# Moving the weight conversion of a fused attention and feed-forward kernel between ScalarE, VectorE and GpSimd, with products of constants at the start

## The chip, the cores and the metric

The kernel runs on one core of one Trainium2 chip. The metric is the device time of one execution in microseconds (us); lower is better. Eleven runs of the kernel before gave a median of 1387.72 us, from 1386.26 to 1390.83 us.

## What is computed

For 8 batches and 8 heads, with 576 tokens and 64 features a head, in float32:

```python
scores = (1/8) * q @ k.T
thresh = max(scores) - tau
scores = where(scores >= thresh, scores, -1e9)
attn   = exp(scores - max(scores)); attn /= sum(attn) + 1e-9
x      = attn @ v              # heads side by side: (8, 576, 512)
xn     = (x - mean(x)) / sqrt(var(x) + 1e-6) * g_ln
out    = x + max(xn @ w_ch1, 0) @ w_ch2    # 512 -> 2048 -> 512
```

The two weights `w_ch1` and `w_ch2` arrive as 64-bit floats (the kernel sees them as 64-bit integers), so the kernel itself turns each of them into float32 before its first use. `g_ln` is multiplied into the rows of `w_ch1`.

## The kernel before, in words

**Slots.** The kernel is one unrolled loop over 72 slots, nine for each batch (`for n in range(NS)`). In a slot, four blocks of 128 x 576 scores are computed on TensorE (`scores`, L393), their negated maxima are taken on VectorE (`exponentials`, L407, two instructions of two blocks), the thresholds are made on GpSimd (L411), the exponentials on ScalarE (L419, four), and VectorE multiplies them with the threshold mask and sums them (`weights`, L426, four, then a reciprocal, L433). The scores lie in two PSUM tiles `sc`, so the scores of the next slot wait for the masks of this one. In the first batch the normalised weights are turned on TensorE with diagonal matrices (`diag` L440 on ScalarE, products `tp` and `tr`, copies `em` and `er` L476 and L499 on ScalarE), and multiplied with v (`pv`, L574 and L584, copied to `x` at L597 and L592). In slots 0 to 2 the next head pair is transposed on VectorE (`turn`, L344, L353, L354, after q was scaled on GpSimd at L341), which waits for the loads of q and k from the SP queue (`load_qk`, L116). Each `tp`, `tr`, `pv`, `p1`, `p2` and `mean` takes one of two PSUM banks of the pool `ps_ff` in turn.

**Feed-forward groups.** The tokens form 16 groups of 288. Group g gets its sums over the heads on GpSimd (`add_feature`, L626), its mean by a product with a constant matrix (`avg_sb`), and its centred x (`xc`, L649, VectorE). Then `first_part` makes 16 hidden tiles of four products each (`p`, then the ReLU `hidden`, L779, on ScalarE), and `second_plain` (group 0) or `second_quarters` (the others) makes the second product. These steps are handed out in four quarters of each slot (`second_part`) by due times, so their place between the attention's products is fixed when the program is built. Group 0 starts at slot 6. In `second_plain`, `add_to_x` multiplies the second product from PSUM with 1/standard deviation on VectorE (L687), and adds x on GpSimd (L688).

**Weight conversion.** The class `Weights` converts 32 chunks of 128 x 512 values: 16 of `w_ch1`, then 16 of `w_ch2`. A chunk has these steps:

- `fetch`: a DMA of 512 KB from the SP queue (L252)
- `begin`: two VectorE instructions on the high words (L272, shift and and; L276, and and or) and two ScalarE instructions (L280, the low word scaled; L284, the square of the high word)
- `carry`: an integer addition of the low word's part on GpSimd (L290)
- `mask`: a VectorE instruction that sets tiny values to zero (L299)
- `end`: for `w_ch1` only, the product with `g_sb` on ScalarE (L312)

The raw and half-made chunks lie in pieces of tiles that are not needed yet (`hidden`, parts of the weights' own room, `et`, `x_room`, `stage`); `piece` and `give` hand them out. One call of `tick` takes one step of each kind: it ends, masks, carries and begins at most one chunk, so a chunk is masked three ticks after its begin. Slots 0 to 2 have two ticks, slots 3 to 5 three, later ones six. `first_part` and `second_plain` do not go on before the chunks that they use have ended.

Of the kernel before, what the change touches and what calls it, by code (L numbers as in the profile page):

```python
# [8 lines left out]
F32 = mybir.dt.float32  # L9
# [9 lines left out]
def kernel(  # L19
# [155 lines left out]
    class Weights:  # L175
# [13 lines left out]
        def __init__(self):  # L189
            self.chunks = [  # L190
                (w1_sb[i][:, c : c + WC], w_ch1[i * 128 : (i + 1) * 128, c : c + WC], i)
                for c in range(0, DF, WC)
                for i in range(NK)
            ] + [
                (
                    w2_sb[:, m, d : d + 4].rearrange("p d c -> p (d c)"),
                    w_ch2[d * 128 : (d + 4) * 128, m * 128 : (m + 1) * 128].rearrange(
                        "(d p) c -> p d c", p=128
                    ),
                    None,  # L200
                )
                for m in range(NK)
                for d in range(0, ND, 4)
            ]
            self.n1 = NK * (DF // WC)
            self.fetched = self.begun = self.carried = self.masked = self.ended = 0
            self.raw, self.made, self.due, self.ticks = {}, {}, [], 2
            flat = lambda t: t.rearrange("p a b -> p (a b)")

            x_room = ffn.tile([128, NK, TOK], F32, tag="x", bufs=3, name="x_room")  # L210
            stage = self.stage = consts.tile([128, 8, WC], F32, name="stage")
            et = att.tile([128, NB, 128], F32, tag="et", bufs=1, name="et0")

            n1 = self.n1
            self.free = []
            for t, n, before in (
                (w2_sb.rearrange("p m d c -> p (m d) c"), ND // 2, lambda p: n1 + 2 * p),  # L220
                (hidden, 4, lambda p: 10),
                (et, 2, lambda p: 2 * n1),
                (x_room, 1, lambda p: 2 * n1),
                (stage, 4, lambda p: 2 * n1),
            ):
                for p in range(n):
                    self.free.append((before(p), -1, flat(t)[:, p * 2 * WC : (p + 1) * 2 * WC]))
# [34 lines left out]
        def begin(self):  # L262
            i = self.begun
            got = self.piece(i, 1) or self.piece(i, -1)
            if got is None:
                return
            self.made[i] = got
            a, y = got[2][:, :WC], got[2][:, WC:]
            self.begun += 1
            self.due.append(self.ticks + 3)  # L270
            au, hi = a.bitcast(U32), self.words(i, U32)[:, :, 1]
            nc.vector.tensor_scalar(  # L272
                out=au, in0=hi, scalar1=3, scalar2=0x3FFFFFFF,
                op0=ALU.logical_shift_left, op1=ALU.bitwise_and,
            )
            nc.vector.scalar_tensor_tensor(  # L276
                out=au, in0=hi, scalar=0xC0000000, in1=au,
                op0=ALU.bitwise_and, op1=ALU.bitwise_or,
            )
# [4 lines left out]
            nc.scalar.activation(y, self.words(i, F32)[:, :, 1], func=AF.Square)  # L284
# [8 lines left out]
        def mask(self):  # L293
            i = self.masked
            self.masked += 1
            got = self.made[i]
            a, y = got[2][:, :WC], got[2][:, WC:]
            dst, _, gi = self.chunks[i]
            nc.vector.scalar_tensor_tensor(  # L299
                out=dst if gi is None else a, in0=y, scalar=(1.0625 * 2.0**-15) ** 2, in1=a,  # L300
                op0=ALU.is_ge, op1=ALU.mult,
            )
            if gi is None:
                self.ended += 1
                self.give(self.made.pop(i))

        def end(self):
            i = self.ended
            self.ended += 1
            dst, _, gi = self.chunks[i]  # L310
            got = self.made.pop(i)
            nc.scalar.mul(dst, got[2][:, :WC], g_sb[:, gi : gi + 1])  # L312
            self.give(got)

        def tick(self):
            self.ticks += 1
            if self.ended < self.masked:
                self.end()
            if self.masked < self.carried and self.due[self.masked] <= self.ticks:
                self.mask()  # L320
            if self.carried < self.begun:
                self.carry()
            if self.begun < self.fetched:
                self.begin()

    def by_blocks(u):

# [71 lines left out]
    def exponentials(n):  # L399


        neg = small.tile([128, 4], F32, tag="neg", name="neg")
        thr = small.tile([128, 4], F32, tag="thr", name="thr")
        es = e_room[(n + 1) % 2 if n < SLOTS else 0]
        for h in range(2):
            i = slice(2 * h, 2 * h + 2)
            nc.vector.tensor_reduce(  # L407
                out=neg[:, i], in_=pairs[h],
                axis=AXL.X, op=ALU.max, negate=True,
            )  # L410
            nc.gpsimd.tensor_scalar(  # L411
                out=thr[:, i], in0=neg[:, i], scalar1=-1.0, scalar2=low_sb,
                op0=ALU.mult, op1=ALU.add,
            )
        run(n, "copy")
        for i in range(4):
            if i == 2:
                yield es, thr
            nc.scalar.activation(es[:, i], blocks[i], func=AF.Exp, bias=neg[:, i : i + 1])  # L419
# [262 lines left out]
        for fn in now:  # L682
            fn()

    def add_to_x(g, m, p2, rb):
        o = ffn.tile([128, TOK], F32, tag="o", bufs=4, name="o")
        nc.vector.tensor_mul(o, p2, rb)  # L687
        nc.gpsimd.tensor_tensor(out=o, in0=o, in1=groups[g][:, m], op=ALU.add)  # L688
        aside.append(lambda: store(nc.vector, g, m, o))

# [111 lines left out]
    def second_plain(g, rb):  # L802
        for m in range(NK):
            p2 = ps_ff.tile([128, TOK], F32, tag="ff", name="p2")
            for d in range(ND):
                while conversion.ended <= conversion.n1 + 4 * m + d // 4:
                    yield 0, 0
                product(
                    p2, lhsT=w2_sb[:, m, d], rhs=hidden[:, d],
                    start=(d == 0), stop=(d == ND - 1),  # L810
                )
                if d < ND - 1:
                    yield 2, 1
            aside.append(lambda m=m, p2=p2: add_to_x(g, m, p2, rb))
            yield 2, 1

    def second_quarters(g, rb):
# [121 lines left out]
    def run(n, i):  # L939
        for fn, args in later_calls.pop((n, i), ()):  # L940
            fn(*args)
# [41 lines left out]
    if w_ch1.dtype == I64:  # L983
        conversion.fetch(4)
    else:
        for i in range(NK):
            nc.sync.dma_start(out=w1_sb[i], in_=w_ch1[i * 128 : (i + 1) * 128])
            nc.scalar.mul(w1_sb[i], w1_sb[i], g_sb[:, i : i + 1])
        for i in range(ND):
            nc.sync.dma_start(  # L990
                out=w2_sb[:, :, i],
                in_=w_ch2[i * 128 : (i + 1) * 128, :].rearrange("p (m c) -> p m c", m=NK),
            )
        conversion.begun = conversion.carried = len(conversion.chunks)
        conversion.masked = conversion.ended = conversion.begun

    turn(0)
    load_v(1)
    for n in range(NS):
        b, s = divmod(n, SLOTS)  # L1000
        ticks = (1, 3, 4)[: 2 + n // 3] if n < 6 else range(1, 7)

        def tick(i):
            if i in ticks:
                conversion.tick()

        run(n, -3)
        scores(b, s)
        run(n, -2)
        run(n, -1)  # L1010
        rest = exponentials(n)
        es, thr = next(rest)
        run(n, 0)
        conversion.fetch(2)
        run_first(stores)
        second_part(n, 0)
        while drops and drops[0][0] is nc.gpsimd:
# [4 lines left out]
        if (n + 1) % SLOTS < HP and u < len(units):  # L1022
            turn(u)
            if u + 1 < len(units):
                load_qk(u + 1)
        if n < SLOTS + HP:
            run_all(aside)
        tick(1)
        run(n, 1)
        second_part(n, 1)  # L1030
        tick(2)
        blocks_go = by_blocks(b * HP)
        diags = weights(es, thr, blocks_go)
# [81 lines left out]
```

## Time and profile before

One execution was profiled: 1387.0 us by the device's clock, and a span of 1385.2 us from its first to its last instruction, so 1.8 us lie around the span.

| | before |
|---|---|
| median of 11 runs | 1387.72 us |
| profiled execution | 1387.0 us, span 1385.2 us |
| TensorE (PE) busy | 1320.6 us, 95% |
| VectorE (DVE) busy | 928.7 us, 67% |
| ScalarE (ACT) busy | 463.4 us, 33% |
| GpSimd (POOL) busy | 606.5 us, 44% |
| chain of work that ended last | PE 83%, DVE 9% |
| starts of the first maxima of slots 0 to 7 | 14.24, 26.27, 37.74, 50.28, 64.52, 78.52, 92.94, 121.73 us |
| starts of those of slots 8 to 12 | 147.26, 166.64, 191.45, 211.47, 230.75 us |

In the views, PE is TensorE's products and PEld its weight loads, L numbers are lines of the kernel, a row of the timeline gives start, duration, engine, line, operation and tiles, and the bracket at its end the idle time before it with what ended it. A window row gives a stretch of the span, its length, and then busy time and number of instructions of PE, PEld, DVE, ACT and POOL, TensorE's granted clock, the DMA engines' busy share and GB/s. A product of this kernel in float32 leaves several records in the trace.

### The profile page before, as it was taken

The page shows a single profiled execution, that of the slowest core. Times are in us where ns is not written, and L with a number is a line of the kernel's source. Part 1 is how long each engine was busy: PE and PEld are TensorE (multiplying, and loading weights), DVE is VectorE, ACT ScalarE, POOL GpSimd, SP SyncE. Part 2 cuts the span into 40 slices and gives each one's busy share as a digit, 9 for nine tenths or more (in the row PEclk, how much of TensorE's full clock was granted, in tenths as well). Part 3 has the DMA queues.
Part 4 walks back from the last instruction along what each step waited for, and adds up shares of the span by engine and source line. Part 5 has one row for each costly group of instructions (what it writes and reads, how often), then busy time and mean ns, then how long its engine had stood idle before and what let it go on. Part 6 is the DMA issues. An engine that isn't in the chain of part 4 may idle for free.

```text
span 1385.2 us, 40405 instructions
## 1 busy us (share of the span) xinstructions
PE 1320.6 (95%) x17360; PEld 991.3 (72%) x17360; DVE 928.7 (67%) x1638; ACT 463.4 (33%) x1003; POOL 606.5 (44%) x807
## 2 busy tenths in 40 slices
PE   4878989999999999999999999999999999999996
PEld 3655655867768696877869687776868677686966
DVE  5997967676776767657776667757776767766211
ACT  3877613232332323232232323323232323323120
POOL 2444444544443544443444455353444445344313
PEclk8999999999999999999999999999999999999998
DMA  9722355447734576447754476445764476444211
GB/s 230 183 77 72 93 142 152 169 145 183 200 132 167 139 200 173 147 143 190 196 160 147 152 196 188 145 143 154 198 187 136 139 186 187 134 160 136 56 17 18
DMA packets 322019, 206.85 MB, mean 149 GB/s; under 512 B 247984, under 2 KB 279472, under 8 KB 313776
## 3 DMA queue, kind: packets, MB, share of 16 engines
q1 hardware_dynamic: 317072, 203.68, 51.0%
q8 instruction: 136, 2.23, 0.7%
q10 hardware_dynamic: 4736, 0.59, 0.4%
q14 instruction: 43, 0.35, 0.1%
q0 software_dynamic: 32, 0.00, 0.0%
HBM read 120.46 MB, written 83.76 MB: 147 GB/s over the span
## 4 chain that ended last, share of the span: by engine, by line
PE 83%; DVE 9%; issue 2%; DMA 2%; ACT 2%; POOL 1%; SPq 1%; POOLq 0%; DVEq 0%; ACTq 0%
PE p L101 35%; PE seg L101 28%; PE sc L393 9%; PE sc L574 8%; DVE e L426 2%; PE sc L584 2%; DVE neg L407 2%; DMA v_in<-in_v_dram 1%; SPq L116 1%; DVE w L272 1%; DVE w L299 1%; PE tp L101 1%; POOL q_in L341 1%; PE mean L101 0%; PE var L101 0%
## 5 line engine op out<-in xcount | busy, mean ns | idle before, releaser
L101 PE MATMUL p<-xc,w 128*64 128x288 f32 x4096 | 519.9, 409 | 13.1 <-ACT hidden L779 5.7
L101 PEld LDWEIGHTS p<-xc,w 128*64 128x64 f32 x4096 | 288.1, 137 | 222.5 <-issue 16.7
L407 DVE TENSOR_REDUCE neg<-sc 128x2 f32<-128x1152 f32 x144 | 188.7, 1352 | 241.9 <-PE sc L393 241.5
L101 PE MATMUL seg<-hidden,w 128*64 128x144 f32 x3840 | 248.3, 287 | 3.8 <-DVE hidden L847 3.8
L101 PEld LDWEIGHTS seg<-hidden,w 128*64 128x64 f32 x3840 | 234.8, 137 | 15.7 <-issue 7.5
L442 POOL TENSOR_SCALAR e<-e,den 128x576 f32<-128x576 f32 x252 | 193.7, 780 | 114.9 <-DVE den L431 114.9
L411 POOL TENSOR_SCALAR thr<-neg,low_sb 128x2 f32<-128x2 f32 x144 | 42.2, 293 | 452.2 <-DVE neg L407 450.2
L426 DVE SCALAR_TENSOR_TENSOR e<-sc,thr,e 128x576 f32<-128x576 f32 x288 | 222.1, 810 | 16.2 <-POOL thr L411 14.5
L779 ACT ACTIVATE hidden<-p 128x288 f32<-128x288 f32 x256 | 106.4, 416 | 323.6 <-PE p L101 323.5
L419 ACT ACTIVATE e<-sc,neg 128x576 f32<-128x576 f32 x288 | 197.6, 753 | 8.5 <-DVE neg L407 8.5
L516 DVE STREAM_TRANSPOSE et<-e 128x1152 f32<-128x1152 f32 x112 | 153.2, 1374 | 18.2 <-POOL e L442 17.8
L393 PE MATMUL sc<-kT,qT 64*64 64x384 f32 (+3 forms) x2048 | 144.8, 412 | 21.4 <-DVE e L426 11.3
L574 PE MATMUL sc<-em,v_in 128*64 128x128 f32 (+1 forms) x2368 | 129.4, 263 | 0.0
L574 PEld LDWEIGHTS sc<-em,v_in 128*64 128x64 f32 x2368 | 122.8, 137 | 7.8
L393 PEld LDWEIGHTS sc<-kT,qT 64*64 64x64 f32 x2048 | 78.0, 136 | 65.7 <-issue 22.8
L101 PE MATMUL seg<-hidden,stage 128*64 128x144 f32 x1920 | 123.3, 287 | 0.0
L101 PEld LDWEIGHTS seg<-hidden,stage 128*64 128x64 f32 x1920 | 117.6, 137 | 2.9 <-issue 2.9
L597 ACT COPY x<-sc 128x128 f32<-128x128 f32 x120 | 31.7, 266 | 251.6 <-PE sc L393 184.7
L847 POOL TENSOR_TENSOR hidden<-hidden 128x576 f32<-128x576 f32 x60 | 84.7, 1426 | 47.8 <-ACT hidden L779 38.2
L862 ACT COPY part<-seg 128x288 f32<-128x288 f32 x75 | 30.2, 403 | 198.4 <-PE seg L101 194.3
L847 DVE TENSOR_TENSOR hidden<-hidden 128x576 f32<-128x576 f32 x60 | 49.2, 854 | 49.1 <-PE seg L101 39.1
L101 PE MATMUL seg<-hidden,e 128*64 128x144 f32 x960 | 65.3, 286 | 0.0
(152 smaller groups left out, 1114.7 us busy)
## 6 DMA issues: line engine op xcount, KB each, us to landing
scr<-et SPq DMA_DIRECT2D x63, 1152.0 KB, 4.9
em<-scr SPq DMA_DIRECT2D x63, 1024.0 KB, 5.7
out_dram<-ot SPq DMA_DIRECT2D x256, 36.0 KB, 3.7
q_in<-in_q_dram SPq DMA_DIRECT2D x124, 72.0 KB, 2.6
k_in<-in_k_dram SPq DMA_DIRECT2D x120, 72.0 KB, 2.9
er<-scr SPq DMA_DIRECT2D x126, 64.0 KB, 5.2
v_in<-in_v_dram SPq DMA_DIRECT2D x28, 256.0 KB, 5.4
w<-in_moe_w_ch_dram SPq DMA_DIRECT2D x10, 512.0 KB, 5.9
```

Source lines behind the costliest of these rows:

```text
L101: nc.tensor.matmul(out[r], lhsT=lhsT[:, r], rhs=rhs, **flags)
L393: nc.tensor.matmul(sc[h][64 * i : 64 * i + 64, at : at + n], lhsT=ql[r] if s == HP else qT[r, half, j * 128 + 64 * i : j * 128 + 64 * i + 64],
L407: nc.vector.tensor_reduce(out=neg[:, i], in_=pairs[h], axis=AXL.X, op=ALU.max, negate=True,)
L411: nc.gpsimd.tensor_scalar(out=thr[:, i], in0=neg[:, i], scalar1=-1.0, scalar2=low_sb, op0=ALU.mult, op1=ALU.add,)
L419: nc.scalar.activation(es[:, i], blocks[i], func=AF.Exp, bias=neg[:, i : i + 1])
L426: nc.vector.scalar_tensor_tensor(out=es[:, i], in0=blocks[i], scalar=thr[:, i : i + 1], in1=es[:, i], op0=ALU.is_ge, op1=ALU.mult, accum_o ...
L442: nc.gpsimd.tensor_scalar(out=es[:, i], in0=es[:, i], scalar1=den[:, i : i + 1], scalar2=1.0, op0=ALU.mult, op1=ALU.mult,)
L516: nc.vector.transpose(et[:, :, 64 * h : 64 * h + 64].rearrange("p n (j c) -> p j n c", j=2), es[:, 2 * h : 2 * h + 2].rearrange("p j (n c) ...
L574: nc.tensor.matmul(dst[64 * h : 64 * h + 64], lhsT=vt[:, h, c, :], rhs=pick(em[:, 2 * j : 2 * j + 2, c], h), start=c == 0 and first, stop= ...
L597: nc.scalar.copy(x_of(2 * b + (s > HP))[:, s % (HP + 1), 128 * j : 128 * j + 128], pv[j])
L779: nc.scalar.activation(hidden[:, d], p1, func=AF.Relu)
L847: eng.tensor_tensor(out=out[at], in0=in0[at], in1=in1[at], op=op)
```

## The change

1. **Order of the conversion.** `tick` is gone. Each slot has a row in the table `BEGUN` with three counts: how many chunks may have begun ahead of the masks of the scores, behind them, and at the slot's end. All chunks begun are carried, masked or scaled together at fixed places of the slot. Slots 0 to 5 begin two chunks each, slots 6 to 8 six each, slot 9 the rest. Before, 15 chunks had begun by the end of slot 5, now 12.
2. **The product with g** moves from ScalarE (L312) to GpSimd (`scale`): a few behind the additions ahead of the masks, and the others between the two threshold instructions of a slot.
3. **Products of constants** on TensorE (`constants`) stand in front of the scores of slots 0 to 4: 22, 26, 8, 8 and 8 products of `avg_sb` and `ident`, into a bank of `ps_ff`, and nobody reads them.
4. **Loads.** In the first four slots two chunks are fetched a slot, behind the loads of q and k; from slot 4 on up to three at two places of a slot (before: two at two places in all slots, the first of them ahead of q and k).
5. **Group 0's second product** is copied from PSUM by ScalarE, and multiplied on VectorE from the copy.

The order of instructions on TensorE is otherwise the same, and from slot 11 on all engines have the same order of instructions as before.

```diff
-        def end(self):
-            i = self.ended
-            self.ended += 1
+        def scale(self):
+            i = self.scaled
+            self.scaled += 1
             dst, _, gi = self.chunks[i]
             got = self.made.pop(i)
-            nc.scalar.mul(dst, got[2][:, :WC], g_sb[:, gi : gi + 1])
+            nc.gpsimd.tensor_scalar(
+                out=dst, in0=got[2][:, :WC], scalar1=g_sb[:, gi : gi + 1], scalar2=1.0,
+                op0=ALU.mult, op1=ALU.mult,
+            )
             self.give(got)
-        def tick(self):
+        def begin_to(self, most):
             self.ticks += 1
-            if self.ended < self.masked:
-                self.end()
-            if self.masked < self.carried and self.due[self.masked] <= self.ticks:
-                self.mask()
-            if self.carried < self.begun:
-                self.carry()
-            if self.begun < self.fetched:
-                self.begin()
+            while self.begun < min(most, self.fetched):
...
+        def carry_all(self):
+            while self.carried < self.begun:
+                self.carry()
+        def mask_all(self):
+            while self.masked < self.carried:
+                self.mask()
+        def scale_all(self):
+            while self.scaled < min(self.masked, self.n1):
+                self.scale()
...
+            if h == 0:
+                conversion.scale_all()
...
-    def add_to_x(g, m, p2, rb):
-        o = ffn.tile([128, TOK], F32, tag="o", bufs=4, name="o")
-        nc.vector.tensor_mul(o, p2, rb)
+    def add_to_x(g, m, o, rb):
+        nc.vector.tensor_mul(o, o, rb)
...
+            o = ffn.tile([128, TOK], F32, tag="o", bufs=4, name="o")
+            nc.scalar.copy(o, p2)
...
+    BEGUN = [
+        (0, 0, 2), (3, 3, 4), (5, 5, 6), (7, 7, 8), (9, 9, 10), (11, 11, 12),
+        (14, 16, 18), (20, 22, 24), (26, 28, 30), (32, 32, 32),
+    ]
+    def constants(times):
+        warm = ps_ff.tile([128, QH], F32, tag="ff", name="warm")
+        for _ in range(times):
+            product(warm[:, :128], lhsT=avg_sb, rhs=ident, start=True, stop=True)
+    constants(22)
...
-        ticks = (1, 3, 4)[: 2 + n // 3] if n < 6 else range(1, 7)
+        masks_at, behind_at, end_at = BEGUN[min(n, len(BEGUN) - 1)]
         run(n, -3)
+        if 0 < n <= HP:
+            constants(8 if n > 1 else 26)
         scores(b, s)
...
-        conversion.fetch(2)
+        if n >= HP:
+            conversion.fetch(3)
...
+        if n < HP:
+            conversion.fetch(2)
...
-        tick(1)
+        conversion.mask_all()
+        conversion.begin_to(masks_at)
+        conversion.carry_all()
+        conversion.scale_all()
         run(n, 1)
         second_part(n, 1)
-        tick(2)
         diags = weights(es, thr, blocks_go)
...
-        tick(3)
+        conversion.mask_all()
+        conversion.begin_to(behind_at)
         run(n, 2)
         second_part(n, 2)
-        tick(4)
+        conversion.carry_all()
...
-        conversion.fetch(2)
-        tick(5)
+        if n >= HP:
+            conversion.fetch(3)
+        if n >= HP + 2:
+            conversion.mask_all()
         run(n, 3)
         second_part(n, 3)
-        tick(6)
+        conversion.begin_to(end_at)
+        conversion.carry_all()
```

More of the change, by code (lines that the diff above doesn't have):

```diff
@@ L205, in __init__ @@
             self.n1 = NK * (DF // WC)
-            self.fetched = self.begun = self.carried = self.masked = self.ended = 0
-            self.raw, self.made, self.due, self.ticks = {}, {}, [], 2
+            self.fetched = self.begun = self.carried = self.masked = self.scaled = 0
+            self.raw, self.made, self.ticks = {}, {}, 2
             flat = lambda t: t.rearrange("p a b -> p (a b)")
@@ L269, in begin @@
             self.begun += 1
-            self.due.append(self.ticks + 3)
             au, hi = a.bitcast(U32), self.words(i, U32)[:, :, 1]
@@ L303, in mask, with ended @@
             if gi is None:
-                self.ended += 1
                 self.give(self.made.pop(i))
-        def end(self):
-            i = self.ended
-            self.ended += 1
+        def scale(self):
+            i = self.scaled
+            self.scaled += 1
             dst, _, gi = self.chunks[i]
             got = self.made.pop(i)
-            nc.scalar.mul(dst, got[2][:, :WC], g_sb[:, gi : gi + 1])
+            nc.gpsimd.tensor_scalar(
+                out=dst, in0=got[2][:, :WC], scalar1=g_sb[:, gi : gi + 1], scalar2=1.0,
+                op0=ALU.mult, op1=ALU.mult,
+            )
             self.give(got)
-        def tick(self):
+        @property
+        def ended(self):
+            return self.scaled if self.scaled < self.n1 else max(self.masked, self.n1)
+        def begin_to(self, most):
             self.ticks += 1
-            if self.ended < self.masked:
-                self.end()
-            if self.masked < self.carried and self.due[self.masked] <= self.ticks:
+            while self.begun < min(most, self.fetched):
+                was = self.begun
+                self.begin()
+                if self.begun == was:
+                    break
+        def carry_all(self):
[3 more added lines that the diff above has]
+            while self.masked < self.carried:
                 self.mask()
-            if self.carried < self.begun:
-                self.carry()
-            if self.begun < self.fetched:
-                self.begin()
+        def scale_all(self):
+            while self.scaled < min(self.masked, self.n1):
+                self.scale()
     def by_blocks(u):
@@ L813, in second_plain @@
                     yield 2, 1
-            aside.append(lambda m=m, p2=p2: add_to_x(g, m, p2, rb))
+            o = ffn.tile([128, TOK], F32, tag="o", bufs=4, name="o")
+            nc.scalar.copy(o, p2)
+            aside.append(lambda m=m, o=o: add_to_x(g, m, o, rb))
             yield 2, 1
@@ L994 @@
         conversion.begun = conversion.carried = len(conversion.chunks)
-        conversion.masked = conversion.ended = conversion.begun
+        conversion.masked = conversion.fetched = conversion.begun
+        conversion.scaled = conversion.n1
+    BEGUN = [
[7 more added lines that the diff above has]
+    constants(22)
     turn(0)
@@ L1000 @@
         b, s = divmod(n, SLOTS)
-        ticks = (1, 3, 4)[: 2 + n // 3] if n < 6 else range(1, 7)
-        def tick(i):
-            if i in ticks:
-                conversion.tick()
+        masks_at, behind_at, end_at = BEGUN[min(n, len(BEGUN) - 1)]
         run(n, -3)
+        if 0 < n <= HP:
+            constants(8 if n > 1 else 26)
         scores(b, s)
```

## The prediction, made before the result was known

> **What bounds the kernel now.** I read first the page's busy shares in 40 slices (34.6 us each), then TensorE's own waits after 250 us.
>
> ```profile
> PE   4878989999999999999999999999999999999996
> DVE  5997967676776767657776667757776767766211
> ```
>
> ```profile
> PE p L101 <- ACT part L862: 4.6, 8, 0.6
> PE seg L101 <- DVE hidden L847: 3.8, 6, 0.6
> ```
>
> From the eighth slice on TensorE is full, and after 250 us it waits 8.4 us in 1135 us. The change leaves the order of those instructions alone, so they cannot win back or lose a start that comes earlier or later: what the first twelve slots save reaches the end. So next I cut the trace into slots, from one slot's first maximum to the next one's (slots 2 to 7).
>
> ```profile
> 37.74:50.28 12.54, 10.79 (x164) 8.33 (x162) 11.77 (x23) 10.63 (x23) 4.93 (x6) 1.00 1.00 242
> 50.28:64.52 14.24, 11.06 (x170) 8.63 (x168) 14.10 (x22) 13.00 (x27) 6.43 (x6) 1.00 0.70 203
> 64.52:78.52 14.00, 9.56 (x146) 7.24 (x142) 13.86 (x21) 11.51 (x25) 6.38 (x6) 1.00 0.12 40
> 78.52:92.94 14.42, 9.95 (x190) 7.61 (x192) 14.28 (x26) 11.69 (x26) 8.45 (x11) 1.00 0.24 75
> 92.94:121.73 28.79, 24.77 (x254) 15.29 (x252) 20.05 (x30) 19.52 (x38) 12.07 (x11) 0.94 0.32 102
> 121.73:147.26 25.53, 24.66 (x308) 17.12 (x310) 25.01 (x40) 18.34 (x38) 9.55 (x8) 1.00 0.15 45
> ```
>
> The third number after the length and PE's and PEld's is VectorE: 14.10 of 14.24 us, so VectorE bounds slots 3 to 5. Its timeline there, with GpSimd's beside it, shows why.
>
> ```profile
> 62.00 1.59 POOL L290 TENSOR_TENSOR w<-w 128x512 int32<-128x512 int32 x1 [1.18 <-ACT w L284]
> 62.34 1.53 DVE L272 TENSOR_SCALAR w<-w 128x512 uint32<-128x512 uint32 x1
> ...
> 67.65 0.42 DVE L272 TENSOR_SCALAR hidden<-w 128x512 uint32<-128x512 uint32 x1
> 68.08 1.29 POOL L290 TENSOR_TENSOR w<-w 128x512 int32<-128x512 int32 x1
> 68.10 1.82 DVE L276 SCALAR_TENSOR_TENSOR hidden<-w,hidden 128x512 uint32<-128x512 uint32 x1
> ```
>
> The same shift takes 0.42 us alone and 1.53 us behind an addition on GpSimd; L276 takes 0.69 us alone and 1.82 us beside one. In slot 6 ScalarE is late for TensorE:
>
> ```profile
> 104.97 2.16 PE L101 MATMUL p<-xc,w 128*64 128x288 f32 x16 [1.00 <-ACT hidden L779]
> 109.90 2.58 PE L101 MATMUL p<-xc,w 128*64 128x288 f32 x10 [2.77 <-ACT hidden L779]
> ```
>
> **What the Trainium skill says.** "SBUF — State Buffer", section "SBUF: two separate sides": VectorE and GpSimd share one pair of ports as an exclusive lock, held for a whole instruction, which VectorE takes in its two-port modes or with two SBUF inputs. The trace agrees (0.42 against 1.53 us). "VectorE: DVE Perf Modes", "Why PSUM operands drop a tier": an operand in PSUM rules the two-port mode out, so maxima and masks should not collide; in the trace the mask at 20.58 us takes its usual 0.81 us while an addition runs from 20.07. "TensorE: Matmul & The Clock Gate", Part 1: the clock halves after about 3.4 us without work and returns after as much sustained work. The trace agrees roughly: the scores of slot 0 take 4.12 us, later ones 2.12; the granted clock is 0.50 from 18 to 28 us (idle since 14.2) and again near 110 us, after 2.77 us idle.
>
> **The change, part by part.** Starts are those of a slot's first maxima; before they are 14.24, 26.27, 37.74, 50.28, 64.52, 78.52, 92.94 and 121.73 us.
>
> *Constants' products, slots 0 and 1.* A product is 4 records, so 88 stand ahead of the first scores. At the half clock (12 records in the us from 27) they take 7.3 us, from 2.4 us (identity ready) to 9.7 at most; the scores wait for qT until 10.1 anyway. Cost 0, gain 4.12 - 2.12 = 2.0 us: slot 0 starts at 12.2. Then 104 records take some 6 us, 12.2 to 18.3, in TensorE's idle time. In slot 0 no chunk begins ahead of the masks (1.03 us less): 2.5 (maxima) + 2.0 (transposes with their wait) + 3.1 (masks, reciprocal) end at 19.8, and two begins of 1.05 beside the scores make slot 1 start at 22.0.
>
> *Loads.* q and k of the next pair no longer queue behind two chunks on SP, but can start only when the transposes have read the old ones, and took 7 to 8 us to issue and 3 to land. I take 1.3 us of wait in slot 1 (bounds 0 and 2.5) and 0.7 in slot 2, as before. Slot 1: 2.5 + 1.3 + 2.0 + two L299 1.25 + begin 1.05 + 3.1 + scores 1.9 = 13.1, slot 2 starts at 35.1. Slot 2: 2.5 + 0.7 + 2.0 + 0.6 + 1.05 + 3.1 + 1.9 = 11.9, slot 3 starts at 47.0: 3.3 us earlier. From slot 4 on six chunks a slot are fetched (3.1 MB, 11 us at the 283 GB/s of the trace's second 10 us); the DMA engines are busy 0.12 to 0.24 there, so 0. SP waits in order for free pieces (24.3 us from 92.7 on), and v of the next batch queues behind; it is needed three slots later: 0.
>
> *Slots 3 to 5.* VectorE loses one chunk of three a slot (0.43 + 0.61 + 0.60 = 1.65 us) and the collisions, of which the trace has 3, 3 and 2 at 1.1 us. 14.2 - 1.65 - 3.3 leaves 9.3 us, so another chain ends last: ScalarE's. In slot 2 it took 8.7 us from the reciprocal (36.0) over diagonals, em and er to the last exponential (44.7); with the last mask that is 9.6 us a slot. L312 leaves this queue (0.6 us each), which gives no more than that. Two things are added to it. The 32 constants' records ahead of the scores of slot 4 (1.9 us) come behind pv (end 9.3 behind the reciprocal) and the scores need 2.0 more: slot 3 takes 11.1 us. (Ahead of slots 2 and 3 VectorE is later anyway: 0. The constants take a bank of `ps_ff` that er's copy frees at 7.5 us, ahead of pv's end: 0.) And L299 behind the masks now takes the chunk begun ahead of them, whose addition needs L280, which stands on ScalarE behind the last exponential: 0.6 + 1.3 us, so L299 and the next begin end 2.7 us behind the masks, where the scores need 1.9: slot 4 takes 10.7. Bounds of this wait: 0 and 2 us a slot. In slot 5 the centring follows x's copies, three sums and the mean: 11.6. Slot 6 then starts at 47.0 + 11.1 + 10.7 + 11.6 = 80.4, or 12.5 us earlier.
>
> *Slot 6.* ScalarE has four chunk steps of 1.15 us ahead of and behind the diagonals, instead of three with L312 (1.75 each). ReLU 2 comes 12.1 us into the slot (before 11.6; TensorE idle 1.45, before 1.0), ReLU 3 at 15.9 (before 16.5; idle 1.8, before 2.8). That gains 0.6 us; the gaps no longer reach 2.8 us, so I take it that the clock stays up (20 records took 4.3 us where 2.5 are due): 1.8 more. 26.4 us instead of 28.8.
>
> *Slots 7 to 10.* TensorE bounds them (24.66 of 25.53). Twenty chunks instead of 17 come here, 8 us of VectorE, which has 25.01 busy in slot 7; but 8 us of collisions in slots 7 to 9 should shrink, and the next maxima have some 17 us until their masks are needed, so I cost it at nothing. If that cover is gone it is up to 8 us. The scaling costs 0.66 us a chunk on GpSimd (L341: 0.74 for 576 columns), 10.6 in all; four of them delay the second threshold of slot 7 by 2.7 us, while VectorE has 3.3 of chunk work to do. Four copies of 0.4 us (L862's price) go to ScalarE, 30% busy there, and free a bank earlier: one wait of 0.7 goes. With the 0.85 us of waits in slot 7 I take 0.9 saved.
>
> Sum: 12.5 + 2.4 + 0.9 = 15.8 us. Against the profiled execution (1387.0 us: span 1385.2 and 1.8 around it) that is 1371.2; against the median of 1387.7, which is 0.7 above, 1371.9, so 1372.
>
> **The rivals.** *A: the mask's wait replaces the collisions.* L299 waits for the addition, that for ScalarE, in slots 1 to 8. For it: ACT is in order, with 13.0 of 14.24 us busy. At 2 us in each of slots 1 to 5 instead of 1 in one, 9 us are lost, 6.8 stay: 1381. *B: slower, by the clock.* If the constants' products do not raise the clock, they hold up the scores: 10.3 us at the half rate of 0.117 us a record to 12.7, then 12.2 us more, and slot 1 starts at 33 us, 6.7 late. Each following slot would run some 20 us of half-clock work (PE 10 to 11 busy), 6 to 7 above before until slot 4: +25 at slot 4, of which 10 come back later: 1402. It decides if the clock is not full by about 24 us. Against it: 0.94 in the us from 28 after 5 us of work. *C: no change.* Late weights in slots 7 to 10: the three chunks moved there and their waits cost TensorE all 15 us. Against it: chunk 15 is scaled 4.4 us into slot 7, and its product comes 14 us in. 1387.
>
> **Chances.** The forecast's case 0.74 (1365 to 1379), A 0.14, C 0.03, B 0.09. Faster by over 0.2% (about what a measurement of this kernel can tell from no change): 0.88, same 0.03, slower 0.09. The forecast's low end takes the loads at 0 (2 us), no wait of L299 (1), a clean end of slots 7 to 10 (2) and 2 us of spread in slots 3 to 5; the high end the reverse, a clock that drops in slot 6 (1.8), and A: 1365 to 1382.
>
> **What would show it.** Right: L272 and L276 at 0.42 and 0.69 us nearly everywhere in slots 1 to 5; slot 0 at 12, slot 6 at 80 and slot 7 at 107 us; granted clock 1.00 from 10 us on, near slot 6 too; the same waits of TensorE after 250 us. Wrong: a half clock at 20 us; idle time of VectorE ahead of L299 with GpSimd's L290 as its end of several us a slot; TensorE waiting for GpSimd's scaling in slot 7; GpSimd's thresholds late for L426.

## The result, and the profile after

The changed kernel takes 1380.4 us (median of 12 runs, 1377.6 to 1382.8), the kernel before 1387.4 us (47 runs, 1384.6 to 1390.8): a ratio of 0.9949, 95% interval 0.9941 to 0.9958. That is 7.1 us faster, where 15.8 were forecast. The profiled execution of the changed kernel took 1377.6 us (span 1375.6), the shortest of the twelve.

The page's busy shares of the changed kernel, in 40 slices of 34.4 us:

```profile
PE   7989989999999999999999999999999999999996
DVE  6988958676765777576766667657776767666211
```

TensorE is busier in the first slices, and nearly full from the seventh on as before. TensorE's waits after 250 us, changed kernel:

```profile
PE p L101 <- ACT part L880: 4.6, 8, 0.6
PE seg L101 <- DVE hidden L865: 3.8, 6, 0.6
```

These are the same 8.4 us as before, so the difference arises ahead of 250 us. The windows of slots 3 to 6, changed kernel:

```profile
47.67:58.86 11.19, 10.59 (x184) 9.02 (x182) 9.72 (x18) 9.11 (x20) 6.29 (x7) 1.00 0.86 324
58.86:69.62 10.76, 9.72 (x152) 7.60 (x148) 9.95 (x19) 8.91 (x19) 6.45 (x7) 1.00 0.71 227
69.62:82.73 13.11, 10.72 (x206) 8.27 (x202) 11.07 (x22) 9.61 (x22) 8.84 (x13) 1.00 0.44 140
82.73:109.62 26.89, 23.58 (x258) 15.09 (x260) 19.35 (x30) 16.14 (x33) 13.13 (x12) 1.00 0.01 2
```

VectorE has 9.72 us to do in slot 3 where it had 14.10, and the slot is 3 us shorter. Its timeline in slot 4, with GpSimd's, shows what is left of the collisions:

```profile
61.99 0.42 DVE L271 TENSOR_SCALAR w<-hidden 128x512 uint32<-128x512 uint32 x1
62.45 0.69 DVE L275 SCALAR_TENSOR_TENSOR w<-hidden,w 128x512 uint32<-128x512 uint32 x1
...
67.05 1.22 POOL L310 TENSOR_SCALAR w<-hidden,g_sb 128x512 f32<-128x512 f32 x1
67.71 0.84 DVE L271 TENSOR_SCALAR hidden<-hidden 128x512 uint32<-128x512 uint32 x1
68.24 0.91 POOL L643 TENSOR_TENSOR sum<-sum,x 128x256 f32<-128x256 f32 x1
68.59 1.11 DVE L275 SCALAR_TENSOR_TENSOR hidden<-hidden 128x512 uint32<-128x512 uint32 x1
```

The begin ahead of the masks now runs alone (0.42 and 0.69 us). Of the one behind them, L271 runs beside the scaling that moved to GpSimd (L310) and L275 beside an addition for the heads' sum (L643): each takes 0.4 us more than alone, where it was 1.1 us more beside L290. TensorE in slot 6 of the changed kernel, its two long waits:

```profile
95.78 2.16 PE L101 MATMUL p<-xc,w 128*64 128x288 f32 x16 [1.53 <-ACT hidden L795]
99.47 2.65 PE L101 MATMUL p<-xc,w 128*64 128x288 f32 x20 [1.53 <-ACT hidden L795]
```

They are 1.53 us each, where they were 1.00 and 2.77. The starts of a slot's first maxima, by slot, in us:

| | 0 | 1 | 2 | 3 | 4 | 5 | 6 | 7 | 8 | 10 | 12 |
|---|---|---|---|---|---|---|---|---|---|---|---|
| before | 14.24 | 26.27 | 37.74 | 50.28 | 64.52 | 78.52 | 92.94 | 121.73 | 147.26 | 191.45 | 230.75 |
| changed | 12.21 | 22.03 | 35.89 | 47.67 | 58.86 | 69.62 | 82.73 | 109.62 | 135.08 | 181.27 | 221.18 |
| earlier by | 2.0 | 4.2 | 1.9 | 2.6 | 5.7 | 8.9 | 10.2 | 12.1 | 12.2 | 10.2 | 9.6 |
| forecast | 12.2 | 22.0 | 35.1 | 47.0 | 58.1 | 68.8 | 80.4 | 106.8 | | | |

So in this pair of executions 12.2 us were won by slot 8, and 2.6 of them were given back in slots 8 to 11.

TensorE's waits there that differ, in slots 7 to 10, first the kernel before, then the changed one:

```profile
131.53 6.71 PE L101 MATMUL p<-xc,w 128*64 128x288 f32 x52 [0.64 <-ACT hidden L795]
177.64 1.09 PE L101 MATMUL tp<-diag,e 128*64 128x128 f32 x16 [0.70 <-DVE o L687]
195.19 0.71 PE L101 MATMUL mean<-sum,avg_sb 128*64 128x288 f32 x4 [1.20 <-POOL sum L626]
201.33 4.59 PE L101 MATMUL p<-xc,w 128*64 128x288 f32 x36 [1.07 <-DVE xc L649]
```

```profile
120.52 6.80 PE L101 MATMUL p<-xc,w 128*64 128x288 f32 x52 [1.74 <-ACT hidden L811]
185.00 0.71 PE L101 MATMUL mean<-sum,avg_sb 128*64 128x288 f32 x4 [2.84 <-POOL sum L643]
191.75 4.59 PE L101 MATMUL p<-xc,w 128*64 128x288 f32 x36 [1.68 <-DVE xc L666]
```

The second of the first four, the wait for a bank, is gone; the other three have grown by 1.1, 1.6 and 0.6 us.

### The profile page after: what moved, and what is told of

Read it like the earlier page. It is cut to its first block, busy times and chain, and to the rows that moved or that the text cites. A ratio compares the mean times of both kernels' runs of the same rounds, so it can differ in the third digit from the quotient of the medians.

```text
span 1375.6 us, 40994 instructions
## 1 busy us (share of the span) xinstructions
PE 1329.4 (97%) x17648; PEld 1005.9 (73%) x17648; DVE 919.3 (67%) x1638; ACT 455.1 (33%) x991; POOL 616.3 (45%) x823
## 4 chain that ended last, share of the span: by engine, by line
PE 84%; DVE 7%; DMA 2%; ACT 2%; POOL 2%; issue 2%; SPq 1%; POOLq 0%; DVEq 0%; ACTq 0%
PE p L101 34%; PE seg L101 28%; PE sc L408 9%; PE sc L591 8%; PE sc L601 2%; DVE e L443 1%; DVE neg L422 1%; DVE w L298 1%; PE tp L101 1%; ACT e L436 1%; DMA v_in<-in_v_dram 1%; DVE w L275 1%; POOL sum L643 1%; PE mean L101 1%; POOL q_in L356 1%
## 5 line engine op out<-in xcount | busy, mean ns | idle before, releaser
L408 PE MATMUL sc<-kT,qT 64*64 64x384 f32 (+3 forms) x2048 | 139.5, 404 | 4.9 <-DVE e L443 3.9
```

The source lines that it names most:

```text
L408: nc.tensor.matmul(sc[h][64 * i : 64 * i + 64, at : at + n], lhsT=ql[r] if s == HP else qT[r, half, j * 128 + 64 * i : j * 128 + 64 * i + 64],
```

## The experiments

Theory 1: the last chunk's late fetch gives time back in slot 9, the load of slot 1's k takes the constants' gain, and TensorE's gaps of 2 to 3 us cost a stretch of half clock in some executions, so that the profiled execution looks better than the median. The rivals are named with each run. The runs were taken in three groups, on three chips, each with its own runs of the kernel before, whose medians were 1388.7, 1388.0 and 1387.4 us. So medians of one group can be set side by side, and those of different groups only by the ratio to the kernel before. All runs, group by group (the first four, the next four, the last four):

| run | median (range) us | ratio to before, 95% interval |
|---|---|---|
| again: the changed kernel | 1380.8 (1377.1 to 1382.4) | 0.9938 (0.9926 to 0.9949) |
| fetch_first | 1376.7 (1375.3 to 1379.0) | 0.9917 (0.9904 to 0.9929) |
| no_constants | 1380.0 (1379.5 to 1381.7) | 0.9942 (0.9931 to 0.9954) |
| before_constants | 1390.3 (1387.1 to 1392.7) | 1.0009 (1.0002 to 1.0017) |
| k_scalar | 1381.5 (1381.0 to 1383.7) | 0.9954 (0.9940 to 0.9967) |
| scale_var | 1380.1 (1376.4 to 1384.9) | 0.9941 (0.9923 to 0.9959) |
| three_a_slot | 1382.8 (1379.0 to 1385.7) | 0.9957 (0.9942 to 0.9972) |
| all_four | 1377.9 (1377.0 to 1379.2) | 0.9926 (0.9911 to 0.9941) |
| late_v | 1378.2 (1376.5 to 1380.9) | 0.9936 (0.9921 to 0.9950) |
| fill_mean | 1378.3 (1377.3 to 1382.5) | 0.9940 (0.9925 to 0.9956) |
| best | 1374.6 (1374.0 to 1375.9) | 0.9911 (0.9895 to 0.9926) |
| best_cold | 1379.4 (1375.9 to 1380.3) | 0.9938 (0.9922 to 0.9954) |

**The changed kernel again** (no edit).

> The changed kernel once more, unaltered. Its twelve runs so far go from 1377.6 to 1382.8 us while the mean granted TensorE clock goes from 0.997 to 0.993, and 0.004 of 1376 us is 5.5 us. Theory 1 (the clock is lost at a place of its own, in some executions): again a median near 1380.4, each run's time following its clock by about 1.2 us for 0.001. Rival (the 2.8 us between the profiled run and the median are spread of DMA transfers): the times vary as much at an unchanged clock.

Measured: two runs near 1377.2 us at a mean clock of 0.997, three near 1380.8 at 0.994, one of 1382.4 at 0.993. The time follows the clock, as theory 1 has it. The profiled execution is the last of these, and its trace shows the place. First the mean and the product behind it in the earlier trace of the changed kernel, then in this one:

```profile
185.00 0.71 PE L101 MATMUL mean<-sum,avg_sb 128*64 128x288 f32 x4 [2.84 <-POOL sum L643]
185.54 4.54 PE L101 MATMUL p<-hidden,w 128*64 128x288 f32 x36
```

```profile
186.46 0.71 PE L101 MATMUL mean<-sum,avg_sb 128*64 128x288 f32 x4 [2.88 <-POOL sum L643]
187.00 6.22 PE L101 MATMUL p<-hidden,w 128*64 128x288 f32 x36
```

The same 36 records behind the same gap take 4.54 us in one execution and 6.22 in the other: 1.7 us, with a granted clock of 0.54 from 187 to 190 us. The second trace has two more such stretches, one behind gaps of 1.37 and 0.61 us ahead of the scores of slot 2, and one behind a gap of 1.97 us in slot 12, where 52 records take 8.21 us, and 6.53 behind the same gap (1.98 us) in the earlier trace.

**The last chunk's fetch ahead of scr.**

```diff
         box = []
         if blocks_go:
+            conversion.fetch(3)
             scr = turn_blocks(s, es)
```

> The last chunk's fetch of slot 9 is issued ahead of the weights' copy (scr) on SyncE's queue instead of behind it; nothing else differs. Theory 1: the last chunk then lands some 5 us earlier, VectorE's wait of 6.67 us at L271 goes, the maxima of slot 10 start right behind the scores (1.7 us earlier), TensorE's wait for the sum falls from 2.84 us to about 1.2 and the one for xc from 1.68 to about 1.1: 2.2 us less, 1378.2. If TensorE's gap of 2.8 us is also where some executions lose their clock, the clock is 0.997 in nearly all runs and the median falls by 2.5 us more, to about 1375.7. Rival (the give-back of slots 8 to 10 is VectorE's additional chunk work): under 0.5 us, 1380.

In the changed kernel the chunk stands on SyncE's queue behind the weights' copy, which waits for VectorE's transposes (SPq rows), and VectorE waits for it:

```profile
172.83 0.36 SPq L538 DMA_DIRECT2D scr<-et  x1
173.28 0.39 SPq L252 DMA_DIRECT2D stage<-in_moe_w_ch_dram  x1
...
179.83 0.43 DVE L271 TENSOR_SCALAR stage<-stage 128x512 uint32<-128x512 uint32 x1 [6.67 <-DMA stage<-in_moe_w_ch_dram]
```

With the fetch first (slot 9 starts 1.9 us later here):

```profile
168.62 0.57 SPq L252 DMA_DIRECT2D stage<-in_moe_w_ch_dram  x1
174.73 0.36 SPq L538 DMA_DIRECT2D scr<-et  x1
...
174.99 0.38 DVE L271 TENSOR_SCALAR stage<-stage 128x512 uint32<-128x512 uint32 x1
```

No wait is left at L271, slot 9 takes 23.8 us instead of 25.4, the wait for the sum falls from 2.84 to 1.2 us, and the median is 4.1 us below the changed kernel's of the same group. Of these 1.6 are the wait; the rest fits the clock, which in this trace has no half stretch from 180 to 200 us. The rival is out. One part of the expectation missed: the wait for xc stays at 1.7 us, since the last chunk's mask (L298, 0.65 us) still stands ahead of the masks of slot 10.

**TensorE kept busy in that gap.**

```diff
+        if g == 1:
+            constants(10)
         means[g] = ps_ff.tile([128, TOK], F32, tag="ff", name="mean")
```

> The changed kernel with ten more of the constants' products (40 records, 2.3 us) ahead of the mean of slot 10, where TensorE waits 2.84 us for the sum: the wait of the mean itself stays, only TensorE is busy in it. Theory 1 (in most executions the clock is halved for some 3.4 us behind this gap, which costs 1.7 us): the mean starts as before, no half clock between 180 and 200 us, and the median falls by 1 to 1.5 us, to 1379 to 1379.5. Rival (the clock falls there by chance and not through the gap, or the constants delay the mean): no change or slower, 1380.5 to 1382.

```profile
181.59 2.35 PE L101 MATMUL warm<-ident,avg_sb 128*64 128x128 f32 x40
184.59 0.71 PE L101 MATMUL mean<-sum,avg_sb 128*64 128x288 f32 x4 [0.65 <-POOL sum L643]
```

The mean still waits for the same sum, and slot 9 is as long as before (25.42 us, 25.40 in the changed kernel), but the 36 records behind the mean take 4.54 us. The median, 1378.3 us, is not clear evidence: it comes from another group than both medians of the changed kernel, and the ratio, 0.9940, lies between its two (0.9949 and 0.9938). The traces decide. All twelve profiles of the changed kernel and its variants have this mean and the 36 records behind it:

| traces | wait ahead of the mean, us | the 36 records, us |
|---|---|---|
| changed kernel | 2.84 | 4.54 |
| again, no_constants, k_scalar | 2.88, 2.80, 2.79 | 6.22, 5.53, 6.10 |
| scale_var, three_a_slot, late_v | 3.51, 3.19, 2.78 | 6.22, 6.98, 5.43 |
| fetch_first, best, best_cold, all_four | 1.19, 1.19, 1.19, 1.20 | 4.54 each |
| fill_mean | 0.65 | 4.54 |

Behind a wait of 2.8 us or more there is a half clock in six traces of seven, behind a shorter one in none of five, and `fill_mean` shortens nothing but TensorE's idle time. So it is the gap on TensorE behind which the clock falls here, and chance decides in which executions. The rival is out by the traces; what the filling is worth in the median stays open.

**No constants' products.** The calls of `constants` are taken out.

> The changed kernel without any of the constants' products (its output stays the reference's). Theory 1: the scores of slots 0 and 1 run at half the clock again, slot 0 starts at 14.2 us instead of 12.2, slot 1 at 25.5 to 26 instead of 22.0; what is behind the k load of slot 1 loses only a part, and the three groups of 32 records ahead of the scores of slots 2 to 4 gave back about 1 us: 2 to 4 us slower, 1382.4 to 1384.4. Rival (the clock of the first two slots is worth nothing since VectorE and the loads bound them): within 1 us of 1380.4.

Slot 0 starts at 13.76 us and slot 1 at 24.71, 1.5 and 2.7 us later than with them; slot 2 starts at 37.22, which is within the 34.9 to 37.9 of the six traces with the same order up to there, and slot 6 at 85.25, where the four of them with nothing else changed ahead of it have 82.3 to 84.6. The median does not show even that (1380.0 against 1380.8 in the same group): the rival is right for the end time. Its trace shows also what the small groups do. Without them TensorE waits 1.04 and 0.61 us ahead of the scores of slot 3, these run at half clock (28 records take 3.46 us, at full clock 2.16), and slot 3 takes 12.6 us instead of 11.2. Slot 4 takes 10.3 instead of 10.8: there, by the difference, the group costs 0.4 us.

**The constants alone, in the kernel before.** `constants` is added to it with the same counts at the same places.

> The kernel before with the constants' products alone (22 ahead of the first turn, 26 ahead of the scores of slot 1, 8 ahead of those of slots 2 to 4). Theory 1: the gain of slots 0 and 1 (2.0 and 2.2 us by the changed kernel's starts) carries through the slots that VectorE bounds, less about 1 us for the small groups: 2 to 4 us faster, 1383.4 to 1385.4. Rival (in the order of before the next pair's loads, queued behind two chunks, or the three chunks a slot hide it): no change, 1387.4; in that case the larger part of the gain belongs to the two chunks a slot and the moved fetches.

It is slower, by 0.09% (interval 0.02 to 0.17%): neither expectation. Slots 0 and 1 start 2.0 and 2.3 us earlier, slot 2 no earlier (37.75), slots 3 to 6 start 1.4 to 2.0 us later. VectorE's two waits, against one of 0.67 us in the kernel before:

```profile
30.34 0.78 DVE L344 STREAM_TRANSPOSE kT<-k_in 128x576 f32<-128x576 f32 x1 [3.74 <-DMA k_in<-in_k_dram]
43.68 0.78 DVE L344 STREAM_TRANSPOSE kT<-k_in 128x576 f32<-128x576 f32 x1 [3.31 <-DMA k_in<-in_k_dram]
```

The lead is spent waiting for the loads. This trace also tests the forecast's clock in slot 6: below the row of the kernel before, then that of this one.

```profile
109.90 4.34 PE L101 MATMUL p<-xc,w 128*64 128x288 f32 x20 [2.77 <-ACT hidden L779]
```

```profile
111.91 2.65 PE L101 MATMUL p<-xc,w 128*64 128x288 f32 x20 [2.76 <-ACT hidden L779]
```

The same wait is followed by a half clock in one and not in the other; slot 6 takes 27.1 us here, not 28.8.

**The k of slot 1 on ScalarE's queue.**

```diff
-                load_qk(u + 1)
+                load_qk(u + 1, (nc.sync, nc.sync if n else nc.scalar))
```

> The changed kernel with one load moved: the k of the pair that slot 1 turns is issued on ScalarE's queue (idle from 16.2 to 20.1 us) instead of behind q on SyncE's. Theory 1 (the constants' gain of slots 0 and 1 is lost in the wait for this load, 2.5 to 2.7 us in three profiles): the wait of kT in slot 1 goes, slot 2 starts 1.5 to 2 us earlier (33.9 to 34.4 instead of 35.9), and TensorE's gap ahead of the scores of slot 2, behind which two of three profiles show a half clock near 37 us, becomes shorter; 1 to 2 us of it reach the end: 1378.5 to 1379.5. Rival (the next pair's load is late in its place): a wait at kT or qT in slot 2 instead, the end within 0.5 us of 1380.5.

```profile
15.61 7.89 ACTq L116 DMA_DIRECT2D k_in<-in_k_dram  x4
...
25.71 0.78 DVE L359 STREAM_TRANSPOSE kT<-k_in 128x576 f32<-128x576 f32 x1 [1.01 <-DMA k_in<-in_k_dram]
29.33 0.77 DVE L368 STREAM_TRANSPOSE qT<-q_in 128x256 f32<-128x256 f32 x2 [2.84 <-POOL q_in L356]
```

The rival, in its mechanism: k lands 1.6 us earlier (kT at 25.71 us instead of 27.28), and slot 2 starts at 37.28, no earlier than in the changed kernel. The four issues take 7.9 us and hold up the diagonals and the chunk steps behind them on ScalarE, so GpSimd's additions, the scaling of q behind them and qT come late in k's place. Another queue was no way past the busy DMA engines. The Trainium skill has it so ("DMA: Bandwidth & Descriptors", section "Issuing engines are not separate DMA queues": transfers started by different engines run on the same 16 DMA engines); the DMA engines' busy share here is 1.00 from 15 to 20 us and 1.10 from 20 to 25. The page calls the time to start a transfer usually small beside the transfer; 7.9 us for four is not.

**Fewer loads ahead of it.**

```diff
-        conversion.fetch(4)
+        conversion.fetch(2)
...
-    load_v(1)
...
                 load_qk(u + 1)
+                if n < HP - 1:
+                    load_v(n + 1)
...
-            conversion.fetch(2)
+            conversion.fetch(2 if n else 4)
...
-        if b == 0 and s < HP - 2:
-            load_v(s + 2)
```

> The changed kernel with other loads in front: two chunks instead of four ahead of the first slot, and the second, third and fourth pair's v each behind the next q and k on SyncE's queue instead of ahead of them. Theory 1 (the DMA engines, busy in full from 10 to 30 us, set the landing of slot 1's k at 27.2 us, whichever queue issues it): with 0.5 MB of chunks and one v fewer ahead, q and k land 2 to 3 us earlier, the waits of kT and qT in slot 1 fall from 2.6 us to under 0.7, and slot 2 starts at 33.5 to 34.5 instead of 35.9 to 37.3; 1.5 to 2.5 us faster than the changed kernel: 1378 to 1379. Rival (another load is late in its place, now v, a chunk or the k of slot 2): slot 3 starts no earlier than 47.5, the end within 0.7 us of 1380.6.

VectorE's waits for loads and q in slots 1 and 2:

```profile
25.83 0.77 DVE L368 STREAM_TRANSPOSE qT<-q_in 128x256 f32<-128x256 f32 x2 [0.52 <-POOL q_in L356]
...
37.82 0.78 DVE L359 STREAM_TRANSPOSE kT<-k_in 128x576 f32<-128x576 f32 x1 [0.93 <-DMA k_in<-in_k_dram]
```

The wait for k, 1.7 to 2.8 us in the six traces with the old order, is gone, though 0.93 us come back at the next k. Slot 2 starts at 34.27 and slot 3 at 46.22, ahead of all six (34.9 to 37.9 and 46.7 to 49.7). The median, 1378.2 us, is as expected, but from another group than the changed kernel's, and the ratio does not tell the two apart (0.9936 against 0.9949 and 0.9938). So the traces show that the wait goes; what it is worth at the end this run does not show.

**Slots 5 and 7.**

```diff
         conversion.mask_all()
-        conversion.begin_to(masks_at)
+        conversion.begin_to(masks_at - (n == HP + 3))
         conversion.carry_all()
-        conversion.scale_all()
+        if n != HP + 1:
+            conversion.scale_all()
         run(n, 1)
         second_part(n, 1)
+        if n == HP + 3:
+            conversion.begin()
+            conversion.carry_all()
```

> Two small moves in the changed kernel, far apart: in slot 5 the scaling of GpSimd goes behind the sums that the mean waits for, and in slot 7 the second chunk's steps on ScalarE go behind the variance's (VectorE's order stays). Theory 1: slot 5 takes 1.0 to 1.4 us less (11.7 to 12.1 instead of 13.1), TensorE's wait for the variance in slot 7 falls from 1.74 to about 0.6 us; 2.2 us in all, 1378.3. Rival (slot 5 is long by VectorE's own work and slot 7's wait moves to the next product of p): under 0.7 us.

Slot 5 takes 12.26 us instead of 13.11: nearly the expected. In slot 7 the wait did not go, it moved:

```profile
117.64 4.10 PE L101 MATMUL p<-xc,w 128*64 128x288 f32 x32 [0.62 <-ACT hidden L811]
122.92 2.65 PE L101 MATMUL p<-xc,w 128*64 128x288 f32 x20 [1.17 <-ACT hidden L795]
```

The second chunk's steps now delay a later ReLU on ScalarE, and slot 7 takes 26.0 us instead of 25.5: theory 1 for slot 5, the rival for slot 7. The 0.3 us left of the gain are below what the medians resolve.

**Three chunks a slot** in slots 3 and 4, one in slot 5, five in slot 6.

```diff
-        (0, 0, 2), (3, 3, 4), (5, 5, 6), (7, 7, 8), (9, 9, 10), (11, 11, 12),
-        (14, 16, 18), ...
+        (0, 0, 2), (3, 3, 4), (5, 5, 6), (7, 8, 9), (10, 11, 12), (12, 12, 13),
+        (15, 16, 18), ...
```

> The changed kernel with three chunks instead of two in slots 3 and 4, one instead of two in slot 5 and five instead of six in slot 6; the order of maxima, additions and masks stays. Theory 1 (VectorE's chain sets slots 3 and 4, so that a chunk there costs its 1.65 us of VectorE): slots 3 and 4 take 12.9 and 12.4 us instead of 11.2 and 10.8, slot 5 gets 1 to 1.6 back unless the mean keeps it, slot 6 loses nothing; 1 to 2.5 us slower at the end, 1381.5 to 1383. Rival (the gain is the collisions taken away, and the number of chunks is worth little, since ScalarE's chain sets these slots): within 0.7 us of 1380.5.

Slots 3 and 4 take 13.00 and 12.76 us (1.8 and 2.0 more), slots 5 and 6 take 1.3 and 1.1 less: 1.5 us more from the start of slot 3 to that of slot 7. The ratio of the median, 0.9957, is the highest of the variants, but its interval overlaps with the changed kernel's. By the trace it is theory 1: a chunk in slots 3 and 4 costs what it takes of VectorE.

**Together.** First the four edits, with k on ScalarE's queue; then the fetch, slot 5's scaling and the later loads (`best`); then this one without the constants.

> The earlier fetch of the last chunk, the k load on ScalarE's queue, and the two moves of slots 5 and 7, together. Theory 1: their gains lie one behind another on the path that TensorE ends, so they add: 4 us from the fetch (1376.7 measured), 2.2 from the two moves, 1.5 from the load: 1373, with a clock of 0.997 in most runs. Rival (the gains of slots 1 and 5 are absorbed later, by ScalarE in slot 6): no better than 1375.5.

> The changed kernel with the last chunk's earlier fetch, the scaling of slot 5 behind the mean's sums, and the loads of the run with v behind q and k. Theory 1: 3.5 to 4 us from the fetch (1376.7 measured), 0.9 from the scaling (slot 5 took 12.26 us instead of 13.1), 1.5 to 2.5 from the loads: 1373 to 1375. Rival (slot 6, which ScalarE sets, or a later load absorbs what the loads gain): 1376 to 1377.

> The run of the three edits together, but without any of the constants' products. Theory 1 (their gain of 1.5 us in slot 0 and 1.1 to 1.2 in slot 1 was lost in the wait for slot 1's load alone, and with that wait gone it comes through): 1.5 to 3 us slower than the run with the constants. Rival (the constants are worth nothing wherever the loads land): within 0.7 us of it.

`all_four` gives 1377.9, the rival's number, with both faults in its trace: slot 2 starts at 37.52 us (k's issue), and slot 7 takes 26.06 us. `best` gives 1374.6 us, 0.89% below the kernel before, where the changed kernel is 0.5 to 0.6% below. Without the constants it is 1379.4 in the same group, and slot 6 starts at 84.40 instead of 80.81: once the loads are in time, the constants are worth 3.6 us at slot 6 and 4.8 in the median, more than expected. Of the 3.6 us, 2.4 are there at the start of slot 2, where the six traces with the old loads scatter from 2.3 us earlier to 0.7 later than `no_constants`, and 1.4 arise in slot 3, which without the constants runs in part at half clock here too. Of the 4.8 us a part is clock: the trace without the constants has another half clock in slot 12 (52 records in 8.22 us), the one with them has none.

## Why the prediction was wrong

The direction, the size at each slot's start up to slot 5 (within 0.9 us) and the main mechanism were right: slots 3 to 5 are 7.6 us shorter, and `three_a_slot` measures a chunk there at 1.8 to 2.0 us, where 1.65 was taken. The share of the collisions is argued from busy times and rows, not run alone. The lengths of slots 3 and 4 came out (11.2 and 10.8 us for 11.1 and 10.7), but in part by luck: the forecast gave VectorE 9.3 us there and let ScalarE's chain end last, so that a third chunk of 1.65 us would have fitted into slot 3; it costs 1.8 us. Both chains end there almost together: in the changed kernel the scores of slot 4 end at 58.4 us, and VectorE's last begin at 58.9. The sum, 15.8 us against 7.1, failed in these terms, by the profiled pair:

- *"Slots 7 to 10 ... 0.9 us saved": failed, the largest.* Measured: 2.5 us lost from slot 7 on, so 3.4 us off. The four waits of TensorE behind it, which add up to 2.6 us: 1.1 us because two chunks instead of one stand ahead of the variance on ScalarE in slot 7 (1.74 against 0.64), 1.6 us for the sum behind the late last chunk, 0.6 us for xc (that the chunk's mask, 0.65 us, is the reason fits by its size and was not run), less the 0.7 us bank wait, which did go. The DMA engines' share was rightly read as low; what I costed at nothing was the queue's order, a fetch behind a copy that waits for VectorE.
- *"I take it that the clock stays up ...: 1.8 more": failed as a gain of the change.* A half clock does not always follow the wait of 2.77 us: `before_constants` has the same wait, 2.76 us, and none. The pair of profiles, 9.4 us apart, set an execution with a half clock in slot 6 beside one with none. But both kernels lose clock in some executions and not in others: the shortest, 1384.6 and 1377.6 us, differ by 7.0 us, and both medians lie 2.8 us above. In the groups of runs above the shortest executions of the kernel before, 1384.6 to 1384.9 us, have a mean clock of 0.997, as has the changed kernel's trace without any half clock. How often the kernel before halves its clock in slot 6 is open, since one trace of it was kept.
- *Slot 5: 11.6 us taken, 13.1 measured.* The scaling on GpSimd stands ahead of the sums that the mean waits for: 0.85 us of the 1.5 by `scale_var`. The rest was not taken apart.
- *Loads: 1.3 us taken, 2.64 measured*, just above the bound of 2.5 that I gave (1.7 to 2.8 in the six traces with this order). With it the constants' products, "gain 2.0", were worth nothing measurable at the end.
- *Slot 6: 0.6 us from ScalarE.* Measured 26.9 us against 27.1 without a half clock: 0.2.

Without the clock in slot 6 the forecast is 14.0 us; less 3.4, 1.5, 0.7 for the loads (slot 3 starts at 47.7 instead of 47.0) and 0.4 to 0.5 for slot 6 it is 8, near the 7.0 to 7.1 measured. The last us is not settled.

Of the rivals, A's number (1381) was near but not its mechanism: the changed kernel's trace shows no wait of L298 for an addition in slots 1 to 5, and VectorE's longest wait for GpSimd there is 0.51 us; L298 does wait in slots 6 and 7, 1.18 and 1.81 us. B is out, the scores of slot 0 run at full speed. C named the right slots and a late chunk, at 2.2 us instead of 15.

## What to carry to other kernels

A lead won early is worth only what the next load leaves of it: follow the queue's order, and move the loads together with the work, or the lead turns into a wait. Before a stretch of low clock is counted as a gain, look whether it is in every execution: compare the mean clock of many runs, and the shortest runs of both kernels. Of a step that is moved to an idle engine ask what stands behind it in that engine's order, as the mean's sums did behind the scaling.

## What the runs showed of the hardware

Half clocks followed gaps of TensorE that are shorter than expected. "TensorE: Matmul & The Clock Gate" of the Trainium skill, section "HAM oscillation — how this bites in real kernels", gives as the rule that no idle gap should be longer than about 3.4 us. In the twelve traces of the changed kernel and its variants a half clock follows the gap of 1.97 to 1.99 us in slot 12 in six (52 records take 8.21 instead of 6.53 us), the gap of 2.78 to 3.51 us ahead of the mean in six of seven, and the gaps of 1.53 to 1.76 us in slots 6 and 7 in none. Length alone is not all: gaps of 0.77 to 1.68 us and then 0.61 us close together ahead of a slot's scores were followed by one in six traces, `before_constants` among them. Where TensorE sets the time, one stretch costs 1.7 us. The page's Part 1 says that the observed window runs freely, so that the moment differs from run to run; that fits the two outcomes behind one gap, but no run here shows the window itself.
